# Phase 0 of an expert layer: weight conversions moved to later slots, four more low halves made by ACT and GpSimd

## The chip, the core and the metric

The kernel runs on one core of a Trainium2 chip. The metric is the device time of one execution in microseconds (us); lower is better. The engines are named as the profile names them: PE (TensorE, with PEld for its weight loads), DVE (VectorE), ACT (ScalarE), POOL (GpSimd) and SP (SyncE, which here issues transfers).

## What is computed

An attention in two steps (32 packed queries read keys and values, then the full queries read the packed result) gives 4608 rows of 512 numbers. These go through a mixture of eight experts with the best expert alone:

```python
p_packed = sm_attn(p, k, v)
x = sm_attn(q, p_packed, p_packed)      # 4608 rows of 512
expert_idx = np.argmax(x @ w_gate, axis=1)
for e in range(8):                       # rows of expert e
    h = np.maximum(xe @ w1[e], 0.0)      # 512 -> 1024
    out[mask] = gate_w[mask, None] * (h @ w2[e])
```

## The kernel before, in words

The first part (to about 148 us) is the attention, in an order of steps written out in the string ORDER. It writes the 4608 rows to a buffer `xd` in device memory, and DVE works out the routing: which row goes to which slot. A slot is a block of 128 rows that have one expert. The routing comes in three stages, of which the second (`second_stage`, the steps F of ORDER) assigns slots 11 to 19. Its last steps are on DVE the products `room` (L313, L314), on PE the 27 small products `inv` (L321), and on DVE the tables `gat`, `sca` and `gpl` (L326 to L337). Its products lie in the tiles of the result rows 9, 10 and 11, so that the gathers of these rows have to wait until PE has read them.

The second part runs in phases (`for pi, (gi, c, layer) in enumerate(phases)`). Slots 0 to 18 are the first group. Phase 0 is the first layer for these slots with the first quarter (256 columns) of the hidden layer, phase 1 the second layer for the same quarter, and so on for four quarters; then the second group follows.

In phase 0 there is, for each slot j:

- `gather(j)`: POOL issues an indirect transfer of the slot's 128 rows from `xd` (L431). In phase 0 the gather of slot j + 5 is written at slot j (GA). Slots 0 to 8 are gathered in the attention part.
- `prep(j)`: PE transposes the rows into the PSUM tile `psx` (L446; the pool `pp` has two buffers, which it shares with the routing's `cnt` and `inv`). ACT writes the high half `x[:, 0]`, scaled, in f16 (L448). The low half, the rest that f16 lost, comes in one of two ways. Without `by_pool` DVE makes it from PSUM in one instruction (L453). With `by_pool` ACT copies the scaled rows to the gathered tile `g` (L450), and POOL subtracts (L451). `prep(j + 2)` is written at slot j (PA). Slots 0 to 5 are prepared in the attention part, where XPOOL picks those with `by_pool`; in phase 0 the call is `prep(jn)`, without it.
- `l1(j)`: twelve matmuls into `psa` (L833): for each of four parts of the 512 columns the high rows with both halves of the weights, and the low rows with the high weights. The third matmul of a slot thus needs the low half. ACT makes `u` (L836, five buffers), DVE its f16 half `hs` (L840), and the rest is subtracted by POOL for even slots, by DVE for odd ones (L842). SP transposes `hs` of two slots by a transfer (L847).

The weights of the next phase are brought meanwhile. `w_load` puts one expert's f32 block in one of four staging buffers (SP, L116). `w_convert` makes the high half on ACT (L141) and the low half on DVE (L142), and lets the next load be written. In phase 0 these are the eight blocks of `w2r`, which the second layer of phase 1 reads at an address known at run time only. They are written at the even slots 0 to 14:

```python
if (j - a) % 2 == 0 and conv:
    with after("V", "A"):
        w_convert(*conv.pop(0))
```

`after("V", "A")` puts a conversion behind the last DVE and ACT instruction that the phases have written until then, as a rule the slot's `hs` and `u`. Apart from such bounds the builder orders each engine's instructions itself, by their place in the program and by a timing model of what is ready; each engine then executes its own in that order.

Of the kernel before, what the change touches and what calls it, by code (L numbers as in the profile page):

```python
# [56 lines left out]
"""  # L57
ND = 14
NX = 6
XPOOL = (1, 2, 4, 5)  # L60
GA = 5
NF = 9
MVG = ()
# [18 lines left out]
def packed_attention_moe(ctx, tc, qT, q1, kT, v4, v1, pT, wg, w1, w2, const, out):  # L82
# [21 lines left out]
    def after(*names):  # L104
        stack = ExitStack()
        for n in names:
            if n in last:
                i = last[n]
                stack.enter_context(tc.issue_after(getattr(i, "ins", i)))
        return stack  # L110
# [41 lines left out]
    def part(j):  # L152
        return sum(z <= j for _, z in parts)
# [242 lines left out]
    def run(gen):  # L396
        try:
            while True:
                next(gen)
        except StopIteration as end:  # L400
            return end.value
# [8 lines left out]
    def xplace(j):  # L410

        m = j % NG
        if j < NG or j >= NM:
            return None, m
        return (m or NG), (0 if m == 0 else NG if m == 1 else m - 1)

    def xpool(m):
        return ys if m < NX else xs
# [5 lines left out]
    def gather(j):  # L424
        if NG + NF <= j < NM:
            g = xs.tile([P, DM], F32, tag=f"h{2 * (j - NG - NF)}", name=f"g{j}")
        elif NG <= j < NM:
            g = xpool(xplace(j)[0]).tile([P, DM], F32, tag=f"x{xplace(j)[0]}", name=f"g{j}")
        else:
            g = ytile(j)  # L430
        last["G"] = G.indirect_dma_start(  # L431
            g,
            None,
            xd[0 : STAGES[part(j)][0] * P, :],
            bass.IndirectOffsetOnAxis(ap=at(gats, j), axis=0),
            bounds_check=STAGES[part(j)][0] * P - 1,
            oob_is_err=False,
        )
        raw[j] = g

    def prep(j, by_pool=False):

        g = raw.pop(j)
        ps = pp.tile([P, 4, P], F32, tag="pp", name="psx")
        for k in range(4):
            T.transpose(ps[:, k, :], g[:, P * k : P * k + P], ident)  # L446
        x = xpool(xplace(j)[1]).tile([P, 2, 4, P], F16, tag=f"x{xplace(j)[1]}", name=f"x{j}")
        A.activation(x[:, 0], ps, AF.Copy, scale=xup)  # L448
        if by_pool:
            A.activation(g, ps.rearrange("p k t -> p (k t)"), AF.Copy, scale=xup)  # L450
            last["G"] = G.tensor_tensor(x[:, 1], g.rearrange("p (k t) -> p k t", t=P), x[:, 0], op=ALU.subtract)  # L451
        else:
            V.scalar_tensor_tensor(x[:, 1], ps, xup, x[:, 0], op0=ALU.mult, op1=ALU.subtract)  # L453
        xt[j] = x
# [5 lines left out]
    with ExitStack() as actx:  # L460
# [302 lines left out]
        for op in ORDER.split():  # L763
# [38 lines left out]
            elif op == "P":  # L802
                j = next(ps)
                prep(j, j in XPOOL)
        tot = run(stages["F"]) or tot
# [18 lines left out]
    def l1(j, es, i, alone=False):  # L824

        x = xt[j]
        ps = pm.tile([P, FC], F32, tag="pm", name="psa")
        n = 0
        for k in range(4):
            for xp, wp in ((0, 0), (0, 1), (1, 0)):  # L830
                for e, c, kw in columns(es):
                    w = weights(w1r, e, 2 * FC * k + FC * wp, FC)
                    last["T"] = T.matmul(ps[c], x[:, xp, k, c], w, start=(n == 0), stop=(n == 11), **kw)  # L833
                n += 1
        u = wk.tile([P, FC], F32, tag="u", name="u", bufs=UB)
        last["A"] = A.activation(u, ps, AF.Relu, scale=SH)  # L836
        if i % 2 == 0:
            hs2[0] = wk.tile([P, 2, 2, FC], F16, tag="hs", name="hs", bufs=HSB)
        hs = hs2[0][:, i % 2]
        last["V"] = V.tensor_copy(hs[:, 0], u)  # L840
        name, eng = ("G", G) if j % HPOOL == 0 else ("V", V)
        last[name] = eng.tensor_tensor(hs[:, 1], u, hs[:, 0], op=ALU.subtract)  # L842

        if alone or i % 2:
            n = 1 + i % 2
            h = xs.tile([P, 2, 2, 2, P], F16, tag=f"h{i - i % 2}", name=f"h{j}")
            last["SP"] = nc.sync.dma_start(  # L847
                h[:, 0:n].rearrange("p s i f t -> p (s i f) t"),
                hs2[0][:, 0:n].rearrange("p s i f -> p (s i f)"),
                transpose=True,  # L850
            )
            for k in range(n):
                ht[j - i % 2 + k] = h[:, k]
# [26 lines left out]
    def scatter():  # L880
        j = done.pop(0)
        i = G.indirect_dma_start(  # L882
            out,
            bass.IndirectOffsetOnAxis(ap=at(scas, j), axis=0),
            yt.pop(j),
            None,
            bounds_check=NT * P - 1,
            oob_is_err=False,
        )
        last["out"] = last["G"] = i  # L890
        tc.declare_no_dep(i.ins if hasattr(i, "ins") else i, group="out", reason="each row of the result is written once")
        tc.add_to_no_dep_group("out", i.ins if hasattr(i, "ins") else i)
# [20 lines left out]
    for pi, (gi, c, layer) in enumerate(phases):  # L913
        a, z = GROUPS[gi]
        first, final = pi < 2 or pi in (2 * NCK, 2 * NCK + 1), pi in (2 * NCK - 1, len(phases) - 1)
        if layer == 0 and first:
            regs = []
        conv = list(sets[pi + 1]) if pi + 1 < len(phases) else []
        if pi == len(phases) - 3:
            with after("G"):  # L920
                G.drain(fusable=False)
        with after("T"):
            for j in range(a, z):
                if layer == 0 and first and len(regs) == j - a and j < NW:
                    y = min(z, NW, parts[part(j)][1])
                    values = nc.values_load_multi_w_load_instructions(
                        seis[part(j)][0:1, j - parts[part(j)][0] : y - parts[part(j)][0]],
                        engines=[mybir.EngineType.PE],
                        min_val=0,
                        max_val=(NE - 1) * EBYTES,  # L930
                        skip_runtime_bounds_check_because="clamped on the chip",
                    )[1]
                    bounds = dict(min_val=0, max_val=(NE - 1) * EBYTES, guaranteed_mod_val=0, out_of_modulus=EBYTES)
                    regs += [v.with_bounds(**bounds) for v in values]
                es = [regs[j - a]] if j < NW else [2 * (j - NW), 2 * (j - NW) + 1]
                if layer == 0:
                    if gi == 0 and first:
                        for jn in range(a if j == a else j + GA, min(j + GA + 1, z)):
                            if jn not in raw and jn not in xt:
                                gather(jn)  # L940
                        for jn in range(a if j == a else j + PA, min(j + PA + 1, z)):
                            if jn in raw:
                                prep(jn)
                    l1(j, es, j - a, j == z - 1)
                else:
                    l2(j, es, first, final)
                if pi in (1, 3):
                    next(side, None)

                s = j - a  # L950
                if pi in (2 * NCK - 2, 2 * NCK - 1) and s % 2 == 0 and s:
                    with after("G"):
                        gather(NG + NF * layer + s // 2 - 1)
                if pi in (2 * NCK - 1, 2 * NCK):
                    s += NG * (pi - 2 * NCK + 1)
                    while turned < NM - NG and (turned if turned < NF else 2 * turned - 2 * NF + 7) <= s and turned <= s:
                        prep(NG + turned)
                        turned += 1
                if done and (pi > 2 * NCK or (j - a) % 4 == 1 or pi == 2 * NCK and (j - a) % 4):
                    with after("G"):  # L960
                        scatter()
                if (j - a) % 2 == 0 and conv:
                    with after("V", "A"):
                        w_convert(*conv.pop(0))
                    if todo and (pi != 2 * NCK - 2 or todo[0] in sets[pi + 1]):
                        w_load(*todo.pop(0))
                if pi == 2 * NCK and j % 2 == 1 and j < a + 2 * NSTG:
                    with after("SP"):
                        w_load(*todo.pop(0))
        if pi == 3:  # L970
            run(side)
# [123 lines left out]
```

## Time and profile before

| | us |
|---|---|
| median of three runs | 577.64 |
| lowest and highest run | 574.23, 577.89 |
| the profiled execution | 575.01 |
| its span, first to last instruction | 573.2 |

The span lies within the execution's time; 1.8 us are outside it. Times in the rows below count from the start of the span. In a timeline one row can stand for several instructions of a kind (x4), with the time from the first's start to the last's end; what stands in brackets is the engine's idle time before it and who ended it.

### The profile page before, as it was taken

The numbers are of one execution on the slowest core, as the hardware profiler recorded it, in microseconds if no ns is written. First come the engines' busy times: TensorE is split into PE (matmuls) and PEld (weight loads), VectorE is DVE, ScalarE is ACT, GpSimd is POOL, SyncE is SP. The second block draws the span as 40 slices with busy tenths as digits, with TensorE's granted clock in tenths as the row PEclk, the third lists the DMA queues.
The fourth block names the chain that finished last, engine by engine and source line by source line (L and its number), as shares of the span: only waits on it lengthen the run. The fifth ranks groups of instructions, "written<-read, shape, count | busy, mean of one in ns | idle before, by whom it ended". The sixth has DMA issues, their size and how long they took to land.

```text
span 573.2 us, 14478 instructions
## 1 busy us (share of the span) xinstructions
PE 531.2 (93%) x4543; PEld 362.0 (63%) x4543; DVE 444.7 (78%) x841; ACT 280.5 (49%) x518; POOL 211.6 (37%) x277
## 2 busy tenths in 40 slices
PE   4899998787869999999999999999999999999994
PEld 2566766554658548845864885598468558648841
DVE  1476877989979798998889787754459989998852
ACT  2355475466637685533642452253776426525400
POOL 3265465348455102510230486456202002101374
PEclk9999999888979999999999999999999999999998
DMA  8998967968589965995996699379969969977863
GB/s 314 411 403 301 380 225 253 369 200 290 186 230 244 208 206 129 246 253 173 256 246 226 156 262 262 126 188 217 284 191 286 250 184 212 252 254 185 156 212 117
DMA packets 118618, 136.78 MB, mean 239 GB/s; under 512 B 82895, under 2 KB 95311, under 8 KB 116624
## 3 DMA queue, kind: packets, MB, share of 16 engines
q1 hardware_dynamic: 102832, 107.21, 68.3%
q0 software_dynamic: 5920, 19.14, 10.7%
q10 hardware_dynamic: 9792, 9.44, 4.9%
q8 instruction: 47, 0.77, 0.6%
q14 instruction: 27, 0.22, 0.1%
HBM read 97.49 MB, written 19.14 MB: 203 GB/s over the span
## 4 chain that ended last, share of the span: by engine, by line
PE 79%; DVE 8%; ACT 5%; POOL 3%; issue 2%; DMA 2%; ACTq 0%; SPq 0%; POOLq 0%; DVEq 0%
PE py L865 34%; PE psa L833 32%; PE s L531 3%; PE x L685 3%; PE psx L446 2%; PE s L628 1%; DVE w2r L142 1%; POOL e L650 1%; PE tr L556 1%; ACT a L540 1%; DMA cst<-const 1%; PE pv L586 1%; ACT x L689 1%; DVE e L647 1%; DMA xd<-x 1%
## 5 line engine op out<-in xcount | busy, mean ns | idle before, releaser
L833 PE MATMUL psa<-w1r,x 128*128 (+1 forms) x1968 | 202.7, 273 | 0.4 <-ACT x L448 0.3
L865 PE MATMUL py<-w2r,h 128*128 (+1 forms) x984 | 195.3, 379 | 0.1
L833 PEld LDWEIGHTS <-x 128*128 128x128 f16 (+1 forms) x1968 | 175.3, 100 | 24.3 <-issue 2.3
L842 POOL TENSOR_TENSOR hs<-u,hs 128x256 f16<-128x256 f32 x76 | 65.7, 865 | 251.3 <-DVE hs L840 243.3
L865 PEld LDWEIGHTS <-h 128*128 128x128 f16 (+1 forms) x984 | 87.5, 100 | 101.2 <-issue 2.7
L836 ACT ACTIVATE u<-psa 128x256 f32<-128x256 f32 x148 | 56.6, 383 | 115.0 <-PE psa L833 104.5
L874 DVE SCALAR_TENSOR_TENSOR y<-py,gpl,y 128x512 f32<-128x512 f32 x111 | 82.1, 747 | 20.7 <-PE py L865 19.7
L142 DVE SCALAR_TENSOR_TENSOR w2r<-stage,w2r 128x1024 f16<-128x1024 f32 x56 | 72.6, 1297 | 5.6 <-ACT w2r L141 5.2
L840 DVE CAST hs<-u 128x256 f16<-128x256 f32 x148 | 54.3, 370 | 27.8 <-ACT u L836 20.4
L142 DVE SCALAR_TENSOR_TENSOR w1r<-stage,w1r 128x1024 f16<-128x1024 f32 x53 | 64.5, 1219 | 11.5 <-ACT w1r L141 11.4
L141 ACT ACTIVATE w1r<-stage 128x1024 f16<-128x1024 f32 x53 | 54.9, 1051 | 33.1 <-DMA stage<-w 33.1
L141 ACT ACTIVATE w2r<-stage 128x1024 f16<-128x1024 f32 x56 | 58.7, 1049 | 0.4 <-DMA stage<-w 0.4
L685 PE MATMUL x<-bd,a2T 128*128 128x264 f32 x128 | 39.4, 435 | 4.5 <-ACT x L689 2.2
L448 ACT ACTIVATE x<-psx,xup 128x512 f16<-128x512 f32 x37 | 25.2, 685 | 33.9 <-PE psx L446 32.5
L882 POOL DMA_INDIRECT out_rows<-y,sca x37 | 37.6, 1017 | 10.8 <-DVE y L874 6.3
L842 DVE TENSOR_TENSOR hs<-u,hs 128x256 f16<-128x256 f32 x72 | 36.1, 501 | 2.0
L531 PE MATMUL s<-k,pb 128*64 128x288 f32 x128 | 24.2, 472 | 9.5 <-DMA k<-kT 5.3
L685 PEld LDWEIGHTS x<-bd,a2T 128*128 128x128 f32 x128 | 23.4, 203 | 14.1 <-issue 3.3
L453 DVE SCALAR_TENSOR_TENSOR x<-psx,xup,x 128x512 f16<-128x512 f32 x33 | 24.6, 746 | 6.2 <-ACT x L448 5.9
L871 ACT ACTIVATE y<-py,gpl 128x512 f32<-128x512 f32 x37 | 25.0, 684 | 8.9 <-PE py L865 8.9
L650 POOL TENSOR_TENSOR e<-e,m 128x512 f32<-128x512 f32 (+1 forms) x20 | 19.2, 962 | 16.0 <-DVE m L649 12.0
L431 POOL DMA_INDIRECT y<-xd,gat x19 | 20.9, 1098 | 9.9 <-PE inv L321 4.5
(174 smaller groups left out, 486.9 us busy)
## 6 DMA issues: line engine op xcount, KB each, us to landing
stage<-w SPq DMA_DIRECT2D x112, 512.0 KB, 4.9
v<-v SPq DMA_DIRECT2D x8, 1024.0 KB, 7.5
q<-qT SPq DMA_DIRECT2D x16, 512.0 KB, 8.5
k<-kT SPq DMA_DIRECT2D x7, 1152.0 KB, 8.0
xd<-x ACTq DMA_DIRECT2D x22, 256.0 KB, 4.3
xd<-w2r ACTq DMA_DIRECT2D x14, 256.0 KB, 7.1
h<-hs SPq DMA_TRANSPOSE x76, 5.3
k<-kT SPq DMA_DIRECT2D x2, 576.0 KB, 4.4
```

The lines of the kernel that those rows point to most:

```text
L141: A.activation(hi, src, AF.Copy, scale=SW)
L142: V.scalar_tensor_tensor(lo, src, SW, hi, op0=ALU.mult, op1=ALU.subtract)
L448: A.activation(x[:, 0], ps, AF.Copy, scale=xup)
L531: T.matmul(ps[64 * j : 64 * j + 64, i, 0:288], p_s[:, 2 * g + j, :], k_s[:, 2 * g + j, 288 * i : 288 * i + 288], start=True, stop=True,)
L685: T.matmul(ps, aT[:, g, P * n : P * n + P], bds[b % 3][:, g, :], start=True, stop=True)
L833: last["T"] = T.matmul(ps[c], x[:, xp, k, c], w, start=(n == 0), stop=(n == 11), **kw)
L836: last["A"] = A.activation(u, ps, AF.Relu, scale=SH)
L840: last["V"] = V.tensor_copy(hs[:, 0], u)
L842: last[name] = eng.tensor_tensor(hs[:, 1], u, hs[:, 0], op=ALU.subtract)
L865: last["T"] = T.matmul(ps[c], h[:, hp, f, c], w, start=(n == 0), stop=(n == 5), **kw)
L874: last["V"] = V.scalar_tensor_tensor(y, ps, at(gpls, j), y, op0=ALU.mult, op1=ALU.add)
L882: i = G.indirect_dma_start(out, bass.IndirectOffsetOnAxis(ap=at(scas, j), axis=0), yt.pop(j), None, bounds_check=NT * P - 1, oob_is_err=False,
```

## The change

Two constants and two places. Slots 8, 10, 12 and 14 join those whose low half ACT and POOL make, and `prep` in phase 0 now looks at that list (slots 6, 7, 9, 11, 13 and 15 to 18 are not on it). The eight conversions of phase 0 are written at slots 4, 6, 8, 10, 12, 13, 14 and 15 in place of 0, 2, 4, 6, 8, 10, 12 and 14, each with the load that goes with it.

```diff
-XPOOL = (1, 2, 4, 5)
+XPOOL = (1, 2, 4, 5, 8, 10, 12, 14)
+CONV0 = (4, 6, 8, 10, 12, 13, 14, 15)
...
                             if jn in raw:
-                                prep(jn)
+                                prep(jn, jn in XPOOL)
...
-                if (j - a) % 2 == 0 and conv:
+                if conv and (j - a in CONV0 if pi == 0 else (j - a) % 2 == 0):
                     with after("V", "A"):
                         w_convert(*conv.pop(0))
```

## Rows read from the trace of the kernel before

**Rows 1.** Chain that ended last, phase 0 (start us, us, what).
```profile
153.60 0.10 DVE w2r L142
...
155.01 0.17 DVE new L366
...
156.46 1.32 DVE w2r L142
...
159.47 1.13 DVE w2r L142
160.60 0.46 DVE room L313 x3
```

**Rows 2.** Windows: busy us and counts by engine, granted clock, DMA share, GB/s.
```profile
158.00:160.00 2.00, 0.00 (x0) 0.00 (x0) 2.00 (x7) 0.00 (x0) 0.78 (x1) 1.00 0.60 162
160.00:161.80 1.80, 0.00 (x0) 0.00 (x0) 1.80 (x8) 0.00 (x0) 0.00 (x0) 0.97 0.59 162
161.80:163.00 1.20, 1.13 (x13) 1.12 (x14) 1.20 (x5) 0.00 (x0) 0.00 (x0) 0.50 0.59 171
...
168.00:169.00 1.00, 0.90 (x6) 0.44 (x4) 0.11 (x1) 0.23 (x1) 0.72 (x1) 0.75 0.91 324
...
191.30:217.00 25.70, 25.70 (x140) 12.20 (x138) 21.09 (x58) 20.10 (x28) 0.67 (x1) 1.00 0.70 210
```

**Rows 3.** Timeline of PE, phase 0.
```profile
147.72 8.68 PE L833 MATMUL psa<-w1r,x 128*128 x72
161.87 0.45 PE L321 MATMUL inv<-room,ohr 128*128 128x36 f16 x9 [5.48 <-DVE room L314]
...
171.59 1.58 PE L833 MATMUL psa<-w1r,x 128*128 x13
...
175.20 1.69 PE L833 MATMUL psa<-w1r,x 128*128 x14
...
181.74 0.65 PE L446 MATMUL psx<-cst,y 128*128 128x128 f32 x4 [1.31 <-DVE x L453]
...
187.25 4.16 PE L833 MATMUL psa<-w1r,x 128*128 x34
```

**Rows 4.** Timeline of ACT: slot 4's conversion, slot 8's high half, slot 6's u.
```profile
155.30 1.05 ACT L141 ACTIVATE w2r<-stage 128x1024 f16<-128x1024 f32 x1
...
166.64 0.69 ACT L448 ACTIVATE x<-psx,xup 128x512 f16<-128x512 f32 x1 [0.17 <-PE psx L446]
168.77 0.38 ACT L836 ACTIVATE u<-psa 128x256 f32<-128x256 f32 x1 [1.45 <-PE psa L833]
```

**Rows 5.** Timeline of POOL: first, second and last of ten gathers, then subtractions.
```profile
163.80 1.01 POOL L431 DMA_INDIRECT y<-xd,gat  x1 [4.51 <-PE inv L321]
165.12 1.00 POOL L431 DMA_INDIRECT y<-xd,gat  x1 [0.30 <-issue]
...
176.81 1.00 POOL L431 DMA_INDIRECT y<-xd,gat  x1 [0.31 <-issue]
177.83 2.10 POOL L842 TENSOR_TENSOR hs<-u,hs 128x256 f16<-128x256 f32 x3
```

**Rows 6.** Line 451 (duration ns min/median/max, first and last start us).
```profile
L451 POOL TENSOR_TENSOR x<-y,x x4: 1154/1203/1995, 139.7 to 148.9; 128x512 f16<-128x512 f32 x4
```

**Rows 7.** Tile gat: time to landing of the nineteen gathers.
```profile
DMA to landing us min/median/max: 3.3/4.1/5.8
```

**Rows 8.** Timeline of DVE, phase 0, single instructions.
```profile
169.19 0.29 DVE L840 CAST hs<-u 128x256 f16<-128x256 f32 x1 [1.08 <-ACT u L836]
170.13 1.22 DVE L142 SCALAR_TENSOR_TENSOR w2r<-stage,w2r 128x1024 f16<-128x1024 f32 x1 [0.65 <-ACT w2r L141]
171.28 0.75 DVE L453 SCALAR_TENSOR_TENSOR x<-psx,xup,x 128x512 f16<-128x512 f32 x1
...
172.36 0.42 DVE L842 TENSOR_TENSOR hs<-u,hs 128x256 f16<-128x256 f32 x1
...
178.71 2.31 DVE L142 SCALAR_TENSOR_TENSOR w2r<-stage,w2r 128x1024 f16<-128x1024 f32 x1
```

## The prediction

> **What bounds the kernel now.** I read the windows first, then the chain of waits, then each engine's timeline around phase 0. From phase 1 on the reader is to see a busy PE: 25.70 of 25.70 us between 191.3 and 217 [rows 2]. So what phase 0 gains or loses goes on to the end in full, and only phase 0 has to be worked out. It lasts from 147.72, the first `psa`, to 187.25 + 4.16 = 191.4 [rows 3], 43.7 us. Its last 34 matmuls take 4.16 us, so its 228 would take about 28 us at that pace. The rest is waiting, and it has two places.
>
> The first is a gap. The six prepared slots are done at 147.72 + 8.68 = 156.4, and PE then waits 5.48 us, until 161.87, for `room` [rows 3]. The chain of waits shows why: the second routing stage runs on DVE, and three conversions stand in it [rows 1]. The gap has an echo. The granted clock is 1.00 until 160, 0.97 up to 161.8 and 0.50 after it, and comes back between 168 and 169 [rows 2]: 1.2 in place of 2.4 GHz for some 6.7 us, after 5.48 us without work.
>
> The second place is the stretch from 170 on, where PE and DVE are both nearly full; one stall of 1.31 us stands out, where a transpose waits for DVE's low half (row at 181.74) [rows 3].
>
> One more fact decides this case. POOL issues the gathers of slots 9 to 18 in one go, ten of them, the first when `inv` is done (163.80), the last at 176.81 + 1.00 = 177.8 [rows 5]. The subtractions for slots 6, 8 and 10 come only after them, at 177.83, although slot 6's `hs` was ready at 169.19 + 0.29 = 169.5 [rows 5, 8]. The builder put all ten gathers ahead of it in POOL's order; its model must take a gather for far shorter than the 1.32 us from one start to the next.
>
> **The change part by part.**
>
> *Two or three conversions leave the routing chain.* On the chain the three cost 155.01 − 153.60 = 1.41, 1.32 and 1.13 us [rows 1]. Those of slots 0 and 2 go for sure: 2.73 us. The third belongs to slot 4 and is still written there. Its high half on ACT ends at 155.30 + 1.05 = 156.35 [rows 4]; without the three conversions `room` would begin at 160.60 − 3.86 = 156.7, so it may or may not slip in again. I take the middle, 3.3 us, with 2.7 and 3.9 as ends. The wait before `inv` shrinks from 5.48 to 2.2 us. The clock was still 1.00 over 158 to 160, up to 3.6 us into the old gap [rows 2], so I let it stay up; the work from 161.87 to 163.80 was done at 0.50, and at full clock it is 0.8 us shorter (ends: 0 and 1.0). The end of `inv`, where the gathers start, moves from 163.8 to 163.8 − 3.3 − 0.8 = 159.7.
>
> *Four low halves leave DVE.* Each took 0.75 us there [rows 8], so 3.0 us. That is about what comes back: the two or three conversions that now fall into the later stretch at 1.22 us each [rows 8], 2.4 to 3.7 us. I count no gain on DVE.
>
> *They arrive on POOL, behind the gathers.* POOL's subtraction takes 1.20 us (1.15 to 2.00) [rows 6], and ACT adds a copy, which its idle time takes in. What counts is the place in the queue. Slot 8's high half was written from 166.64 to 167.33 [rows 4], so its subtraction would have been ready, with a second ACT pass of the same length, at 168.0. That is only 1.5 us before slot 6's `hs`, and that one had all ten gathers ahead of it. So I expect nearly all ten ahead of slot 8's low half too, and all ten ahead of slot 10's, whose rows come two slots later. Ten gathers last 177.8 − 163.8 = 14.0 us: POOL is free at 159.7 + 14.0 = 173.7, and slot 8's low half is there at 174.9, 175.0 with the hand-over. Slot 8's matmuls begin now within the run at 171.59 (its first one ends slot 7), and the third, which needs the low half, at about 172.0 [rows 3]. So PE loses 3.0 us there in spite of the earlier start. The lower bound is no loss, if the builder puts the subtraction between early gathers; the upper 2.00 instead of 1.20 us on POOL, 3.8 us. The Trainium skill, "GPSIMD Engine Reference", Key points, calls VectorE about twice as fast in elementwise work; the rows give 1.20 against 0.75 us, 1.6 times. By that rule, an estimate, the subtraction would take 1.5 us and the sum below be 0.3 us higher, 580.8.
>
> *The clock falls there instead.* By then PE has been without work for long. Gather 9 lands 3.3 to 5.8 us after its issue [rows 7], at 163.0 to 165.5, slot 7's matmuls are done some 2 us later, and then nothing comes until 175.0: about 8 us, more than the 5.48 us that took the clock to 0.50. I give it the same 6.7 us at half speed [rows 2], all of it full of work, and charge half: 3.3 us (ends: 0 and 3.4).
>
> *The rest of phase 0.* From slot 8's third matmul to the end it took 191.4 − 172.0 = 19.4 us. The stall of 1.31 us [rows 3] goes, since DVE catches up while PE waits: 18.1 us. With the clock 21.4 us: phase 0 ends at 175.0 + 21.4 = 196.4, 5.0 us later than now.
>
> *The last four conversions crowd.* Slots 12 to 15 have one each. DVE then has 4 x 1.22 of conversions, 4 x 0.29 of `hs`, 2 x 0.42 of odd subtractions and 3 x 0.75 of low halves (slots 15, 16, 17), 9.1 us [rows 8], in four slots of PE, some 7.2 us (by the stretch from 171.59 to 175.20, two slots with their transposes in 3.6 us [rows 3]). DVE falls 2 us behind. The second layer waits for the whole of `w2r`, and after slot 15 PE has three slots, about 4 us, in which `u`, `hs`, the subtraction and the last conversion take 0.4 + 0.3 + 0.4 + 1.2 us beside those 2. It just fits or just doesn't: 0.5 us (0 to 2). The loads are written later too, but each conversion has five slots or more after its buffer was freed; SP's transposes, which stood behind the loads of slots 0 and 2, move ahead of them and are needed only in phase 1. I count both at nothing; a late load would cost what it is late.
>
> **Sum.** 5.0 + 0.5 = 5.5 us more. The profiled execution took 575.0 us (span 573.2 and 1.8 outside), so 580.5 us. The median of the three runs is 2.6 us above the profiled execution, so a measured median may lie that much higher.
>
> **The rivals.**
>
> *Early place: faster.* If the builder puts the low halves of 8 and 10 between the gathers, as soon as they are ready, PE doesn't wait. For it: they stand before the later gathers in the program. Against it: slot 6's subtraction does too, and came after them [rows 5]. Then the 4.1 us at the front stay whole, the stall may go, and the 0.5 us are paid: −3.6 to −4.9, say −4.2, 570.8 us. It decides as soon as slot 10's low half is done less than about 12 us after `inv` (now its matmuls start there, at 175.2 + 0.3 [rows 3]).
>
> *Half way: no change.* Seven gathers ahead of slot 8's low half, all ten ahead of slot 10's. POOL: 7 x 1.32 + 1.2 + 3 x 1.32 + 0.7 (slot 6's `hs`, a third of 2.10 [rows 5]) + 1.2 = 16.3 us after 159.7, so 176.0, against 175.5 now. From there 191.4 − 175.5 − 1.3 = 14.6 us and 0.5: 191.1, −0.3 us, 574.7 us. Two short waits of PE wouldn't bring the clock down.
>
> *DVE pays for POOL: slower still.* A conversion took 2.31 instead of 1.22 us while POOL subtracted from 177.83 on [rows 5, 8]. If each of the four new subtractions holds DVE up by 1.1 us, 4.4 us stand against the 3.0 saved: 1.4 us more on DVE, and 1.5 us of the crowded end that I counted at 0.5 come as 2: 5.5 + 1.4 + 1.5 = 8.4, 583.4 us. Against it: two of three engines wait at the time. The Trainium skill, "GPSIMD Engine Reference", Key points, says that GpSimd shares its SBUF interfaces with VectorE and contends with instructions of two SBUF inputs; the 2.31 us agree. By that rule alone this rival's 583.4 us would be the likeliest time, since all four subtractions lie beside DVE's work.
>
> *The edit does little.* If slot 4's conversion and others fill the chain's gaps as before, only the POOL part is left; that is the upper end of the sum.
>
> **How the numbers follow.** Forecast 0.45, half way 0.18, early place 0.25, DVE pays 0.12. The range runs from the early place to beyond the sum with DVE's share: 571 to 585 us. The likeliest case has its own range, 576.5 to 584, by its bounds (front 2.7 to 3.9, clock 0 to 3.4, POOL up to 2.0 us). About 1%, 5.8 us, is what a measurement of this kernel can tell from no change. The forecast lies just under it, so over a third of its chance and most of the last rival's make slower, 0.27; the early place reaches −1% at its best only, 0.07; the same 0.66.
>
> **What would show it.** Right: in POOL's timeline L451 for slot 8 after eight or more gathers; in PE's a wait for L451 of 5 us or more before slot 8's or 10's matmuls; a granted clock of 0.50 there and 1.00 where it is 0.50 now; `inv` at about 158.6. Wrong: L451 between the first gathers, no wait of PE on POOL, and the first `py` before 188. The forecast also falls if the clock drops in the first gap as before, or if the wait before the first `py` shows a conversion.

## The result and the profile after

Twenty runs of each kernel on one chip give a median of 580.90 us after and 576.13 us before; the ratio is 1.0085, with a 95% interval from 1.0063 to 1.0106. Two of the changed kernel's runs took 1093 and 1384 us; the ratio leaves out runs that are over 1.5% above the fastest of their kernel. The forecast was 580.5 us, 5.5 us above the profiled execution; the medians differ by 4.8 us. The time and the direction were right. What made them up was partly something else.

The profiled execution took 581.01 us, 6.0 us more than that of before. PE's timeline of phase 0, against [rows 3]:

```profile
151.35 8.72 PE L834 MATMUL psa<-w1r,x 128*128 x72 [0.78 <-issue]
160.47 0.39 PE L322 MATMUL inv<-room,ohr 128*128 128x36 f16 x9 [0.39 <-DVE room L315]
...
165.32 0.63 PE L447 MATMUL psx<-cst,y 128*128 128x128 f32 x4 [2.77 <-DVE tf L328]
...
171.83 0.63 PE L447 MATMUL psx<-cst,y 128*128 128x128 f32 x4 [1.39 <-DMA y<-xd,gat]
...
179.71 1.37 PE L834 MATMUL psa<-w1r,x 128*128 x10 [0.39 <-POOL x L452]
...
190.98 0.66 PE L447 MATMUL psx<-cst,y 128*128 128x128 f32 x4 [1.95 <-DVE x L454]
...
194.00 2.97 PE L834 MATMUL psa<-w1r,x 128*128 x22 [1.06 <-ACT x L449]
196.82 0.59 PE L866 MATMUL py<-w2r,h 128*128 x2
```

Line numbers are one higher than before. Three things are to be seen. Phase 0 begins at 151.35 instead of 147.72, 3.6 us later, ahead of anything that the change touches: up to there each engine executes the same instructions in the same order in both kernels. From the first `psa` to the first `py` it takes 196.82 − 151.35 = 45.5 us, against 43.5 before (first `py` at 191.26 there). And PE's wait for `room` has gone from 5.48 to 0.39 us, while others have come: 2.77, 1.39 (for gathered rows), 0.39, 1.95 and 1.06 us in these rows.

POOL's timeline, against [rows 5]:

```profile
162.17 1.67 POOL L843 TENSOR_TENSOR hs<-u,hs 128x256 f16<-128x256 f32 x1 [2.96 <-DVE th L392]
164.00 1.01 POOL L432 DMA_INDIRECT y<-xd,gat  x1 [0.15 <-issue]
...
176.79 1.00 POOL L432 DMA_INDIRECT y<-xd,gat  x1 [0.31 <-issue]
177.81 0.68 POOL L843 TENSOR_TENSOR hs<-u,hs 128x256 f16<-128x256 f32 x1
178.44 4.49 POOL L452 TENSOR_TENSOR x<-y,x 128x512 f16<-128x512 f32 x4
183.17 1.58 POOL L843 TENSOR_TENSOR hs<-u,hs 128x256 f16<-128x256 f32 x1 [0.23 <-DVE hs L841]
```

This is the order that was forecast: ten gathers, slot 6's subtraction, and then the four new low halves (L452, x4) in one go. The first, slot 8's, comes at 178.4, although ACT had finished that slot's copy at 170.2 (169.50 + 0.69).

The windows show the clock, against [rows 2]:

```profile
164.00:166.00 2.00, 0.68 (x7) 0.68 (x8) 1.94 (x12) 0.02 (x1) 1.70 (x2) 1.00 0.93 236
166.00:168.00 2.00, 2.00 (x13) 1.70 (x11) 0.75 (x1) 0.96 (x3) 1.39 (x3) 0.57 1.01 294
168.00:170.00 2.00, 2.00 (x13) 1.51 (x12) 1.23 (x2) 2.00 (x4) 1.70 (x2) 0.57 1.35 138
...
176.00:178.00 2.00, 1.93 (x18) 1.52 (x17) 0.36 (x1) 1.58 (x3) 1.67 (x3) 1.00 0.80 190
```

It falls to 1.2 GHz for most of 166 to 170, behind the 2.77 us, and stays at 2.4 GHz while the low halves are late: PE is busy for 1.93 of 2 us from 176 to 178.

### The profile page after: what moved, and what is told of

Its sections match the earlier page's. It is cut to its first block, busy times and chain, and to the rows that moved or that the text cites. A ratio compares the mean times of both kernels' runs of the same rounds, so it can differ in the third digit from the quotient of the medians.

```text
span 579.2 us, 14475 instructions
## 1 busy us (share of the span) xinstructions
PE 535.6 (92%) x4543; PEld 364.7 (63%) x4543; DVE 440.4 (76%) x837; ACT 282.5 (49%) x522; POOL 217.3 (38%) x281
## 4 chain that ended last, share of the span: by engine, by line
PE 77%; DVE 7%; DMA 4%; POOL 4%; ACT 3%; issue 3%; ACTq 0%; SPq 0%; POOLq 0%; DVEq 0%
PE py L866 33%; PE psa L834 30%; PE x L686 4%; DMA v<-v 3%; PE s L532 2%; PE s L629 2%; POOL y L432 2%; DMA k<-kT 2%; PE psx L447 1%; POOL e L651 1%; PE bd L604 1%; DVE w2r L143 1%; PE tr L557 1%; PE pv L587 1%; DVE e L648 1%
## 5 line engine op out<-in xcount | busy, mean ns | idle before, releaser
L843 POOL TENSOR_TENSOR hs<-u,hs 128x256 f16<-128x256 f32 x76 | 68.3, 898 | 252.2 <-DVE hs L841 238.8
L841 DVE CAST hs<-u 128x256 f16<-128x256 f32 x148 | 55.7, 379 | 30.6 <-ACT u L837 28.7
L454 DVE SCALAR_TENSOR_TENSOR x<-psx,xup,x 128x512 f16<-128x512 f32 x29 | 21.6, 746 | 11.0 <-ACT x L449 10.9
L432 POOL DMA_INDIRECT g<-xd,gat x18 | 19.9, 1104 | 12.0 <-PE py L866 10.3
```

Of the source, the lines that this page charges most:

```text
L432: last["G"] = G.indirect_dma_start(g, None, xd[0 : STAGES[part(j)][0] * P, :], bass.IndirectOffsetOnAxis(ap=at(gats, j), axis=0), bounds_c ...
```

## The experiments

They ran on three chips, on each of which the kernel of before has a median of 586.0 us; the chip of the first comparison isn't known, and its 576.1 us point to another. Ratios are to the kernel of before on the same chip. The first four rows share a chip, so do the next four and the last four.

| run | what it has | ratio | 95% interval | first `psa` | phase 0, us |
|---|---|---|---|---|---|
| a3_conv | conversions moved | 1.0018 | 0.9991 to 1.0046 | 147.94 | 49.6 |
| a4_pool | low halves on POOL | 1.0051 | 1.0021 to 1.0081 | 149.43 | 51.7 |
| a5_first | both, gathers behind the low halves | 0.9972 | 0.9939 to 1.0004 | 151.40 | 46.2 |
| a2_after | the change again | 1.0063 | 1.0035 to 1.0090 | 151.84 | 50.8 |
| a1_before | before again | 0.9988 | 0.9961 to 1.0016 | 147.64 | 48.5 |
| b3_poolfirst | low halves, gathers behind them | 0.9980 | 0.9947 to 1.0012 | 152.66 | 46.5 |
| b2_spread | conversions at 6 to 13 | 1.0021 | 0.9995 to 1.0046 | 151.80 | 48.7 |
| b1_both | b2_spread with b3_poolfirst | 0.9955 | 0.9926 to 0.9985 | 148.60 | 47.6 |
| c1_broken | before, gathers broken up | 0.9957 | 0.9938 to 0.9976 | 149.01 | 44.3 |
| c2_spread_broken | b2_spread, gathers broken up | 0.9933 | 0.9907 to 0.9959 | 150.55 | 43.1 |
| c3_conv_broken | a3_conv, gathers broken up | 0.9885 | 0.9854 to 0.9917 | 146.66 | 41.6 |
| c4_both_again | b1_both again | 0.9962 | 0.9934 to 0.9990 | 147.46 | 47.4 |

Phase 0 is the stretch from the first `psa` to the first `py` in the one profile of each run.

**The two halves of the change, and the order on POOL.** Each half alone:

```diff
 # a3_conv, against the changed kernel
-XPOOL = (1, 2, 4, 5, 8, 10, 12, 14)
+XPOOL = (1, 2, 4, 5)
```

> The conversions alone at slots 4 to 15; the low halves of slots 8, 10, 12 and 14 stay on DVE. Theory Q (the low halves stand behind ten gathers in POOL's order and cost what the change loses): the front keeps its gain of about 3.4 us and only the crowded end costs up to 2, so phase 0 is 1 to 3 us shorter than the 43.5 us of before and the time 0.2 to 0.6% lower. Theory E (the crowded end and the late load of the last block cost it): phase 0 takes 45 to 46 us as in the changed kernel, time 0.4 to 0.8% higher. Theory A (something ahead of phase 0 became slower by 3 us or more): the first psa comes at 151 us instead of 148.

```diff
 # a4_pool, against the changed kernel
-CONV0 = (4, 6, 8, 10, 12, 13, 14, 15)
+CONV0 = (0, 2, 4, 6, 8, 10, 12, 14)
```

> The four low halves alone on ACT and POOL; the conversions stay at slots 0, 2, ... 14. Theory Q: no gain at the front, and the low halves of slots 8 to 14 come only after the ten gathers, so phase 0 is 3 to 6 us longer than the 43.5 us of before, time 0.5 to 1% higher. Theory E: phase 0 within 1 us of before, since the conversions end as before. Theory A: the first psa at 151 us with the time 0.5% higher.

The low halves alone cost 0.5%, as theory Q said. The conversions alone brought nothing, where Q had expected a gain and E a loss; neither was met (the interval just reaches E's 0.4%).

The third kernel leaves the change as it is and binds the gathers behind the low halves:

```diff
 # a5_first: in prep, with by_pool
-            last["G"] = G.tensor_tensor(x[:, 1], ...
+            last["X"] = last["G"] = G.tensor_tensor(x[:, 1], ...
...
 # in phase 0
-                                gather(jn)
+                                with after("X"):
+                                    gather(jn)
```

> The changed kernel with one more bound: a gather of phase 0 is issued behind the low halves that POOL has been given before it in the program (so slot 8's after three gathers, slot 10's after five, slot 12's after seven, slot 14's after nine). Theory Q: PE no longer meets slots without a low half, phase 0 is 2.5 to 5 us shorter than the changed kernel's 45.5 us, time 0.4 to 0.9% below the changed kernel. Theory E: phase 0 stays at 45 to 46 us, because the last conversions and the load decide. Theory A: the first psa stays at 151 us.

It runs 0.9% below the changed kernel beside it (0.9972 against 1.0063), the upper end of what Q expected. POOL's timeline shows the new order, with two low halves among the gathers:

```profile
166.98 1.00 POOL L432 DMA_INDIRECT y<-xd,gat  x1 [0.30 <-issue]
169.64 0.67 POOL L843 TENSOR_TENSOR hs<-u,hs 128x256 f16<-128x256 f32 x1 [1.66 <-DVE hs L841]
171.41 1.15 POOL L452 TENSOR_TENSOR x<-y,x 128x512 f16<-128x512 f32 x1 [1.10 <-ACT y L451]
172.71 1.02 POOL L432 DMA_INDIRECT y<-xd,gat  x1
174.03 1.00 POOL L432 DMA_INDIRECT y<-xd,gat  x1 [0.30 <-issue]
175.06 1.17 POOL L452 TENSOR_TENSOR x<-y,x 128x512 f16<-128x512 f32 x1
```

Its last gathers now come late: PE waits for rows four times, 4.6 us in all. The changed kernel itself ran beside it:

> The changed kernel once more, for a second profile. If the 3.6 us ahead of phase 0 in the first profile (first psa at 151.35 instead of 147.72) are the loads of one execution, the first psa comes at 147 to 149 this time and phase 0 takes 45 to 46 us; by theory A it comes at 151 again. By the first twenty runs the time is 0.85% above before.

The cost repeats (0.63%). So does the late start: 151.84.

**Is it the order, or the run of gathers?** The kernel of before, the low halves with bound gathers, conversions kept out of the routing chain, and both:

> The kernel of before once more, for a second profile and for the spread: ratio within 0.3% of 1. The first psa comes anywhere between 147 and 152 us, if what lies ahead of phase 0 varies by itself; always near 148, if the change did it (theory A).

```diff
 # b3_poolfirst: a5_first with
+CONV0 = (0, 2, 4, 6, 8, 10, 12, 14)
 # b2_spread: a3_conv with
+CONV0 = (6, 7, 8, 9, 10, 11, 12, 13)
 # b1_both: a5_first with
+CONV0 = (6, 7, 8, 9, 10, 11, 12, 13)
```

> Low halves of slots 8, 10, 12 and 14 on POOL with gathers bound behind them, conversions at slots 0, 2, ... 14 as before. Theory Q: what the same four low halves cost without the bound (0.5%) is gone, 0.2% above to 0.4% below before. Theory E: POOL's order isn't the cost, 0.4 to 0.6% above before.

> Conversions alone, at slots 6, 7, 8, ... 13 and so out of the routing chain altogether; low halves on DVE. Theory E (the gain at the front is lost again where slots 12 to 15 each have a conversion and the last load comes late): the last four come two slots earlier and PE waits less at the end, 0.3 to 0.7% below before. Without it (the front gives nothing because something else holds phase 0): within 0.2% of before, as with the conversions at slots 4 to 15.

> Both mended: conversions at slots 6 to 13, four low halves on POOL with the gathers bound behind them. If Q and E each name a cost of the change, their mends add up: 0.5 to 1.0% below before, phase 0 some 5 us shorter than the 43.5 us of the first profile. If only Q holds, 0.2 to 0.4% below, as with the bound alone.

The bound takes away what the low halves cost (1.0051 to 0.9980). The conversions at 6 to 13 bring nothing by themselves, against E's expectation. Both together gain 0.45%, between the 0.2 to 0.4% that was expected of Q alone and the 0.5 to 1.0% of Q with E. The profile of before on this chip showed why the first chip's reading wasn't enough. ACT's timeline, behind slot 6's `u`:

```profile
171.42 0.38 ACT L836 ACTIVATE u<-psa 128x256 f32<-128x256 f32 x1 [5.34 <-PE psx L446]
171.70 1.05 ACT L141 ACTIVATE w2r<-stage 128x1024 f16<-128x1024 f32 x1
175.66 0.69 ACT L448 ACTIVATE x<-psx,xup 128x512 f16<-128x512 f32 x1 [2.91 <-remote]
177.23 0.38 ACT L836 ACTIVATE u<-psa 128x256 f32<-128x256 f32 x1 [0.88 <-remote]
```

ACT stands idle for 2.91 and 0.88 us, and the profile names no engine that ended it ("remote"). By PE's rows slot 9's transposes, which are all that the instruction at 175.66 waits for, were done at 169.1. POOL issues its ten gathers from 162.56 to 176.2 there. With the conversions at 6 to 13 the same wait is longer, and PE's with it (first ACT, then PE):

```profile
176.62 0.38 ACT L837 ACTIVATE u<-psa 128x256 f32<-128x256 f32 x1 [7.24 <-remote]
```

```profile
179.86 1.16 PE L834 MATMUL psa<-w1r,x 128*128 x4 [9.77 <-ACT x L449]
```

All five profiles on these chips with ten gathers in a row have it; the three with a5_first's bound don't. On the first chip neither profile has it. So there was a new rival, R: the run of gathers itself is what costs.

"Remote" doesn't mean that no engine took part. The profile models the ends of matmuls, but the trace also keeps the updates of the semaphore by which PE reports a finished group, and that is the one that the instruction at 175.66 waits for. Taken in order, the update for slot 9's transposes, whose row ends at 169.08, came at 175.64. In b2_spread the updates for the groups that end at 167.37, 168.49, 169.01 and 170.09 by the rows came at 176.54, 176.65, 176.71 and 176.77. So ACT waited for PE's reports, and these came late.

**The run of gathers, broken up without any low half on POOL.**

```diff
 # c1_broken, against before (c2_spread_broken: b2_spread, c3_conv_broken: a3_conv, each with this)
         last[name] = eng.tensor_tensor(hs[:, 1], u, hs[:, 0], op=ALU.subtract)
+        last[name, j] = last[name]
...
-                                gather(jn)
+                                with after(*[("G", (jn - 8) // 2 * 2)] if jn > 13 else []):
+                                    gather(jn)
```

> The kernel of before, its conversions and low halves untouched, with the run of ten gathers on POOL broken up: gathers 14 and 15 behind the subtraction of slot 6's hs, 16 and 17 behind slot 8's, 18 behind slot 10's. Theory Q (the low halves' place in POOL's order is the cost, nothing else about the gathers): within 0.2% of before. Theory R (a run of ten gathers holds ACT up by itself: on the second chip every profile with such a run had 4 to 7 us of ACT idle in it that no engine explains, the three with a broken run had none): 0.4 to 0.8% below before, and no such wait of ACT.

> Conversions at slots 6 to 13, low halves on DVE, gathers broken up. Theory R: the gain at the front shows at last, 0.6 to 1.0% below before. Theory Q with E: as the conversions at 6 to 13 alone, 0 to 0.3% above before.

> The change's own slots for the conversions (4 to 15), low halves on DVE, gathers broken up. Theory E (the crowded end costs 1 to 2 us): 0.2 to 0.4% slower than the conversions at 6 to 13 with the same gathers. Without E: the same as that kernel within 0.15%.

> Conversions at 6 to 13, low halves on POOL with the gathers bound behind them, a second time: again 0.3 to 0.7% below before. If POOL's low halves themselves bring something (DVE freed), it is 0.2% or more below the kernel with the same conversions, low halves on DVE and broken gathers; if only the broken gathers do, the two are the same.

R holds and Q alone falls: the kernel of before gains 0.43% by this edit alone, with conversions and low halves untouched, and none of the four profiles has a wait of ACT put down to "remote". It isn't gone altogether: in c1_broken ACT still stands 3.87 us before slot 6's `u` (5.34 in a1_before), and PE's report came 3.0 us after the row's end.

```profile
171.55 0.38 ACT L836 ACTIVATE u<-psa 128x256 f32<-128x256 f32 x1 [3.87 <-PE psx L446]
```

Two limits: on this chip no kernel with ten gathers in a row was profiled, and the edit also brings slot 6's subtraction forward. No wait of PE, ACT or DVE in phase 0 of a1_before is put down to a subtraction of `hs` by POOL, so nothing speaks for the second as the cause.

The conversions' gain, which two kernels with ten gathers in a row didn't show, is now there with the change's own slots: 0.9885 against 0.9957, 0.7%. With slots 6 to 13 it isn't clear (0.9933, whose interval reaches 0.9957). E falls too: the change's own slots (4 to 15), with their crowded end, aren't slower than 6 to 13; the ratios have them faster, but their intervals overlap. The low halves on POOL bring nothing (0.9962, no better than 0.9933 with the same conversions). R doesn't explain what the change itself costs, since the kernel of before has the ten gathers too: beside that run the low halves alone cost 0.5% (a4_pool).

c3_conv_broken beats both kernels, by 1.15% against before. POOL's timeline in it:

```profile
164.87 1.00 POOL L432 DMA_INDIRECT y<-xd,gat  x1 [0.30 <-issue]
165.89 1.61 POOL L843 TENSOR_TENSOR hs<-u,hs 128x256 f16<-128x256 f32 x1
167.66 1.02 POOL L432 DMA_INDIRECT y<-xd,gat  x1 [0.16 <-issue]
168.98 1.00 POOL L432 DMA_INDIRECT y<-xd,gat  x1 [0.30 <-issue]
171.55 0.67 POOL L843 TENSOR_TENSOR hs<-u,hs 128x256 f16<-128x256 f32 x1 [1.57 <-DVE hs L841]
```

and PE's, with the waits that are left:

```profile
156.11 0.39 PE L322 MATMUL inv<-room,ohr 128*128 128x36 f16 x9 [0.76 <-DVE room L315]
...
160.97 1.09 PE L447 MATMUL psx<-cst,y 128*128 128x128 f32 x4 [2.77 <-DVE tf L328]
...
184.27 4.14 PE L834 MATMUL psa<-w1r,x 128*128 x32
188.25 0.59 PE L867 MATMUL py<-w2r,h 128*128 x2
```

Slot 6's subtraction comes after five gathers instead of ten. PE still waits 2.77 us for the routing's tables, as in the changed kernel. At the end the 32 last matmuls run without a wait, although slots 12 to 15 have a conversion each, as in the change.

## Why the prediction was right, and where it wasn't

**Conversions leave the chain: right, at the upper end.** `inv` was to begin 3.3 us earlier, counted from the first `psa`; it begins at 160.47 − 151.35 = 9.1 us instead of 14.15, 5.0 earlier. All three conversions left the chain, but 1.0 of the 5.0 us is no gain: in the profile of the change the first `psa` comes late against the routing on DVE as well (DVE's timeline, before and after):

```profile
148.49 1.35 DVE L199 TENSOR_TENSOR ohr<-cst,pos 128x1152 f16<-128x1152 f32 x1
```

```profile
151.15 1.35 DVE L200 TENSOR_TENSOR ohr<-cst,pos 128x1152 f16<-128x1152 f32 x1
```

Counted from this step of the routing, `inv` comes after 9.3 us instead of 13.4, 4.1 earlier, where 3.9 was the upper end. The gain didn't reach the gathers whole. Slot 4's conversion comes right behind, between `inv` and the tables (DVE's timeline):

```profile
162.09 1.21 DVE L143 SCALAR_TENSOR_TENSOR w2r<-stage,w2r 128x1024 f16<-128x1024 f32 x1
...
165.14 0.15 DVE L328 SCALAR_TENSOR_TENSOR tf<-inv,tf 128x9 f32<-128x9 f32 x1
```

and slot 4's subtraction on POOL, which DVE now feeds later, stands ahead of the gathers (162.17, 1.67 us). So the first gather comes 12.65 us after the first `psa` instead of 16.08: 3.4 us earlier, where 4.1 were counted (2.5 us, counted from the routing step).

**Low halves behind ten gathers: right.** Slot 8's was to be there at 174.9, 27.2 us after the first `psa`; it was at 178.44 + 1.1 = 179.6, 28.2 us after it. Without the bound a4_pool costs 0.5%, with it b3_poolfirst nothing. The bound also breaks up the run of gathers, so these two don't part the two causes. c1_broken shows that breaking the run up is worth 0.43% by itself; b3_poolfirst with 0.9980 isn't better than that.

**PE stands still for 8 us and its clock falls: wrong.** This is the step that failed. It put 3.0 us of lost time at slot 8 and 3.3 us on the clock. I had kept PE's order as it was. In the builder's new order PE does the first two matmuls of slots 8 and 10 and finishes slot 9 before them:

```profile
172.30 0.38 PE L834 MATMUL psa<-w1r,x 128*128 x2
...
173.29 0.38 PE L834 MATMUL psa<-w1r,x 128*128 x2 [0.18 <-ACT x L449]
173.95 0.38 PE L834 MATMUL psa<-w1r,x 128*128 x2 [0.27 <-ACT x L449]
...
174.69 1.25 PE L834 MATMUL psa<-w1r,x 128*128 x10
```

(PE's timeline of the changed kernel; two matmuls each of slots 8, 9 and 10, then the ten that slot 9 lacked). PE's wait on POOL is 0.39 us, and the clock stays up from 170 on. The clock fell earlier, behind the 2.77 us, where I had let it stay up. By the prediction's own signs the mechanism fell: no wait of 5 us on POOL, and no clock of 0.50 at slot 8. The second profile of the change, a2_after, does have PE idle for 4.42 us up to 179.25 and a granted clock of 0.50 from 173 to 182, but that wait is for ACT, which stood before PE's late reports; no wait of PE there is for POOL.

**The crowded end and the load: mis-sized in the profile of the change.** I counted 0.5 us, and the loads at nothing. There PE waits 1.95 and 1.06 us. ACT stands 1.71 us before slot 15's conversion, for its load:

```profile
192.27 1.06 ACT L142 ACTIVATE w2r<-stage 128x1024 f16<-128x1024 f32 x1 [1.71 <-DMA stage<-w]
```

But the slots of the conversions aren't to blame by themselves: with the same slots, c3_conv_broken has no such wait. It looks like what becomes of them when the slots before come late together; no run shows that by itself.

**The sum.** Phase 0 is 1.9 us longer in the first pair of profiles and 2.3 us in the second (50.8 against 48.5, on two chips of like time), not 5.5. The 4.8 us of the medians are more than that. In the first pair nearly all of the rest lies ahead of phase 0, in the second 4.2 us ahead of it and 3.1 behind; phase 0 begins at 151.35 and 151.84 with the change and at 147.72 and 147.64 without. I can't call this an effect of the change: the engines' order is the same up to there, and b3_poolfirst begins later still (152.66) but runs at 0.9980. It stays open. That the total came out nearer than its parts was luck.

**The rivals.** *Early place* and *half way* fell with POOL's order. *DVE pays for POOL* had the right mechanism, but mostly on the other engine: four of POOL's subtractions of `hs` took 1.58 or 1.59 us beside DVE's conversions (the first at 183.17), where before one did. The Trainium skill, "GPSIMD Engine Reference", Key points, speaks of such contention; the 1.58 us agree.

## What to carry to other kernels

When a wait is taken out at one place, read from each engine's queue what is issued next and in which order: here the conversions' gain of 0.7% appeared only once the ten gathers behind it were broken up. An order that the builder makes anew with each edit has to be read anew too; an engine that "must wait" may be given other work. And a second profile on another chip is worth its time, since it showed a wait that the first didn't have.

## What the runs showed of the hardware

Ten gathers issued by POOL in a row went with 3.8 to 7.2 us of ACT idle that the profile gives to no engine (or in part to "issue"), in all five profiles on the chips of the experiments and in neither of the first comparison. In each of the five, the most belated of PE's reports in phase 0 came 4.9 to 9.2 us after its matmuls' modelled end; in the seven with the run broken into at most five gathers it was 3.0 us or less, and in the first comparison 0.03 us or less. So a matmul's row can end long before the others learn of it. What held the reports stays open. The traces of the experiments also lack 11 to 24 of PE's 532 to 535 updates, and landing times of the transfers, where those of the first comparison lack no update of PE; whether the recording takes part can't be told. The kernel of before took 1.7% longer on the three chips of the experiments than in the first comparison (586.0 against 576.1 us).
